# Tile fetches declared free of the scatters of rows that they do not read, in a convolution with a mixture of experts

## The chip, the cores and the metric

The kernel runs on one core of one Trainium2 chip. The metric is the device time of one execution in microseconds (us). Before the change, the median of three runs is 1216.68 us (1212.07 to 1216.96).

## What is computed

There are two parts, one behind the other. The first is a convolution over the sequence with a weight of its own for each position: for 8 x 3584 positions, 8 heads of 24 columns and 7 taps, the softmax over the 7 taps weighs the present row and the 6 before it.

```python
w = softmax(weight_gen)                        # (8, 3584, 8 heads, 7 taps)
out[b, s, h] = sum_k w[b, s, h, k] * x_pad[b, s + k, h]     # 192 columns
```

The second is a mixture of 8 experts over the 28672 rows that result. Each row goes to the one expert whose embedding it is closest to.

```python
logits = normalized(x) @ normalized(expert_emb).T / tau
e = argmax(logits);  gate = softmax(logits)[e]
out = gate * (relu(x @ w1[e]) @ w2[e])         # 192 -> 1024 -> 192
```

## The kernel before

**Units and groups.** The 28672 rows come in 32 units of 896 rows (128 partitions x 7 rows). VectorE forms the seven taps of a unit (`taps`), ScalarE squares, scales and splits the rows into two halves of 16 bits (`squares`, `scale`, `split`), and the result lies in one of three buffers `row_0x` to `row_2x`, unit n in buffer n mod 3. SyncE turns the buffer with a transposing DMA (`turn`, tile `xT`), TensorE forms the logits from it, VectorE picks the expert (`choose`), TensorE counts ranks (`ranks`), and VectorE gives every row its place (`places`). Units are routed in 18 groups: the first four have one unit each, the other fourteen two.

**Lists.** In device memory there is a table `lst` with a region for each expert. `scatter` (line 629) writes the rows of a group to their places with indirect DMAs from POOL, 128 rows each: 7 for a unit, 14 for a group of two. Each expert's list only grows: rows of a later group lie above those of an earlier one.

**Tiles.** The rows are then read back sorted by expert. After most groups a batch of eight tiles is planned, one for each expert, of 128 rows ('P') or 256 rows ('T'): the first batch follows group 1 and reads rows of groups 0 and 1, the second follows group 3, and from group 4 on there is one batch a group. That makes 16 batches, 128 tiles; 28 last tiles follow. `schedule` sets the first row of each tile from what has been placed so far. `fetch` (line 687) reads a register with the row, then issues two DMAs from SyncE: a transposing one that brings the rows in as columns (`xt`, three buffers), and a small one for row numbers and gates (`meta`). TensorE multiplies by the first layer (`first`, into `h_ps`), ScalarE and VectorE or TensorE make the rectified halves `hi` and `lo`, TensorE multiplies by the second layer (`second`, into `acc`), ScalarE scales it into `o`, and POOL stores it by row number (`store`).

**Order.** A planner in the program (`run_steps`, line 1029) lays all steps of all engines out in one order by costs and due times that are written down in the configuration. It calls each step's function in that order, and each engine runs its instructions in the order in which they were called. Scatters of a later group stand on POOL in between the stores; fetches stand on SyncE in one queue with the loads of `x_t` and `w_t` and the turns `xT`. SyncE issues one after the other and stops where one has to wait.

**Waits.** The framework draws an edge from an instruction to earlier ones that write what it reads. A scatter and a fetch both address `lst` by a register or by indices, so for the framework each touches the whole table. By hand, scatters are freed of each other and of the fetches (group "rows" and group "loads", lines 640 to 642). A fetch is given edges to the scatters of its batch's groups by hand as well: `deps`, which for a batch holds the scatters of the groups that no earlier batch has taken. Fetches of earlier batches stand ahead of it in the same queue.

Of the kernel before, what the change touches and what calls it, by code (L numbers as in the profile page):

```python
# [24 lines left out]
    groups=(1, 1, 1, 1, 2, 2, 2, 2, 2, 2, 2, 2, 2, 2, 2, 2, 2, 2),  # L25
# [55 lines left out]
def tile_dynconv_moe(  # L81
# [97 lines left out]
    def raw_ins(i):  # L179
        return getattr(i, "ins", i)  # L180
# [51 lines left out]
    rows = [a[:, 0 : U * ROWP].rearrange("p (t r) -> p t r", r=ROWP) for a in packs]  # L232
# [429 lines left out]
    class Tile:  # L662
# [14 lines left out]
        def load_rows(self, row0, deps):  # L677
            def fetch():
                return self.fetch(nc.sync.value_load(row0, min_val=0, max_val=DUMMY))

            for i in SP.behind(fetch):
                i = raw_ins(i)
                tc.add_to_no_dep_group("loads", i)
                for d in deps:
                    tc.add_manual_dep(i, d.name, sync_dep, reason="rows of the lists")

# [410 lines left out]
    groups, group_of = [], {}  # L1097
# [574 lines left out]
```

## Time and profile before

| | |
|---|---|
| median of three runs | 1216.68 us |
| the profiled execution | 1221.34 us |
| its span, first to last instruction | 1219.4 us |
| mean granted TensorE clock | 0.971 |
| TensorE busy | 1120.5 us (92%) |
| VectorE busy | 1035.9 us (85%) |
| ScalarE busy | 812.4 us (67%) |
| POOL busy | 623.2 us (51%) |

In the profile PE is TensorE's matmuls, PEld its weight loads, DVE is VectorE, ACT is ScalarE, POOL is GpSimd, SP or SPq is SyncE's queue. A name such as `xt<-lst` says what an instruction writes and reads. All instructions that pass through the helper that keeps the program's order stand at L66, so they are told apart by their tiles. The time in brackets at the end of a timeline row is the idle time of that engine just before it, with what ended it. "DMA xt<-lst" as the one that ended a wait is the landing of a fetch, "DMA lst<-row_2x,pos" that of a scatter. SyncE itself is never counted as busy, so its rows have no such bracket; its waits have a table of their own.

### The profile page before, as it was taken

To read this page: it belongs to the slowest core of one execution; us is meant where nothing else is said; L and a number is where in the kernel's file an instruction comes from. 1 tells how busy PE (TensorE), PEld (TensorE's weight loads), DVE (VectorE), ACT (ScalarE), POOL (GpSimd) and SP (SyncE) were. 2 spreads that over 40 slices of the span, in tenths; PEclk is the share of its full clock that TensorE was granted. 3 is DMA by queue.
4 is the path that set the end of the run, shared out by engine and by line. 5 is a ranking of instruction groups with operands and counts; after the bars stand their busy time and mean duration, and the time that the engine had idled before them with its cause. 6 is when DMAs were issued, how large, how long until landed. Compare 5 with 4: busy or idle time off the path is not lost.

```text
span 1219.4 us, 34694 instructions
## 1 busy us (share of the span) xinstructions
PE 1120.5 (92%) x13318; PEld 987.5 (81%) x13318; DVE 1035.9 (85%) x1561; ACT 812.4 (67%) x2076; POOL 623.2 (51%) x566
## 2 busy tenths in 40 slices
PE   4888678859999999999999999999999999999994
PEld 2444477748898888888988899889999999899994
DVE  8999979999998999999999999999985363348982
ACT  1678657668897988888898777576666444434442
POOL 3135243637675575857567584738554632222331
PEclk9988889979999999999999999999999999999997
DMA  9979245555565756665666663654444522112110
GB/s 260 261 163 230 60 130 142 139 135 144 141 189 104 182 150 132 168 158 158 165 137 174 140 154 99 158 124 135 95 96 98 141 57 54 49 38 50 46 43 23
DMA packets 254495, 156.15 MB, mean 128 GB/s; under 512 B 225005, under 2 KB 238565, under 8 KB 251248
## 3 DMA queue, kind: packets, MB, share of 16 engines
q1 hardware_dynamic: 228656, 94.86, 36.3%
q0 software_dynamic: 25664, 58.98, 15.6%
q8 instruction: 106, 1.74, 0.6%
q14 instruction: 69, 0.57, 0.2%
HBM read 62.20 MB, written 46.45 MB: 89 GB/s over the span
## 4 chain that ended last, share of the span: by engine, by line
PE 77%; DVE 10%; DMA 6%; ACT 3%; issue 1%; POOL 0%; SPq 0%; POOLq 0%; DVEq 0%; ACTq 0%
PE h_ps L66 40%; PE acc L66 35%; DVE acc_0x L66 2%; DMA xt<-lst 2%; DMA w_t<-in_weight_gen_dram 2%; PE g_ps L66 1%; DVE prod_1x L66 1%; DMA xT<-row_2x 1%; DVE acc_1x L66 1%; DVE prod_0x L66 1%; ACT hi L66 1%; PE sums_a L66 1%; ACT sq L66 1%; DVE sums L66 1%; DMA lst<-row_2x,pos 1%
## 5 line engine op out<-in xcount | busy, mean ns | idle before, releaser
L66 PE MATMUL h_ps<-xt,wall 128*128 128x128 f16 (+2 forms) x5120 | 466.3, 252 | 26.7 <-DMA xt<-lst 22.3
L66 POOL DMA_INDIRECT out_dram<-o,meta x228 | 298.7, 1310 | 367.1 <-ACT o L66 216.3
L66 PEld LDWEIGHTS <-wall 128*128 128x128 f16 (+2 forms) x5316 | 390.7, 99 | 107.2 <-issue 39.9
L66 PE MATMUL acc<-wall,hi 128*128 128x192 f16 x3200 | 410.8, 246 | 0.0
L66 PE MATMUL acc<-wall,lo 128*128 128x192 f16 x1600 | 394.2, 246 | 2.0 <-ACT lo L66 1.9
L66 ACT ACTIVATE hi<-h_ps 128x512 f16<-128x512 f32 x456 | 259.4, 599 | 132.2 <-PE h_ps L66 124.3
L66 PEld LDWEIGHTS <-hi 128*128 128x128 f16 x3648 | 328.7, 98 | 10.5 <-issue 2.8
L66 DVE SCALAR_TENSOR_TENSOR lo<-h_ps,hi 128x512 f16<-128x512 f32 x236 | 154.8, 686 | 113.0 <-ACT hi L66 111.6
L66 ACT ACTIVATE o<-acc,meta 128x192 f32<-128x192 f32 x228 | 88.2, 419 | 166.0 <-issue 148.8
L66 PEld LDWEIGHTS <-lo 128*128 128x128 f16 x1824 | 178.7, 98 | 3.1 <-ACT lo L66 3.1
L66 DVE TENSOR_TENSOR prod_1x<-x_t,w_t 128x1344 f32<-128x1344 f32 x93 | 144.0, 1548 | 0.0
L66 DVE TENSOR_TENSOR prod_0x<-x_t,w_t 128x1344 f32<-128x1344 f32 x93 | 143.9, 1547 | 0.0
L66 ACT ACTIVATE lo<-h_ps 128x512 f16<-128x512 f32 x220 | 127.5, 600 | 10.2 <-PE h_ps L66 9.7
L66 POOL DMA_INDIRECT lst<-row_0x,pos x77 | 102.2, 1328 | 57.3 <-issue 27.5
L66 POOL DMA_INDIRECT lst<-row_1x,pos x77 | 103.2, 1340 | 34.7 <-issue 29.2
L66 POOL DMA_INDIRECT lst<-row_2x,pos x70 | 89.5, 1279 | 49.6 <-issue 48.8
L66 PE MATMUL h_ps<-hi,minus 128*128 128x512 f16 x220 | 73.1, 380 | 5.9 <-ACT hi L66 5.6
L66 DVE TENSOR_TENSOR acc_0x<-acc_0x,prod_1x 128x1344 f32<-128x1344 f32 x45 | 69.8, 1551 | 0.5
L66 DVE TENSOR_TENSOR acc_1x<-acc_1x,prod_1x 128x1344 f32<-128x1344 f32 x45 | 69.6, 1547 | 0.5
L66 DVE TENSOR_TENSOR acc_0x<-acc_0x,prod_0x 128x1344 f32<-128x1344 f32 x45 | 69.8, 1550 | 0.0
L66 DVE TENSOR_TENSOR acc_1x<-acc_1x,prod_0x 128x1344 f32<-128x1344 f32 x45 | 69.6, 1547 | 0.0
L66 PEld LDWEIGHTS <-xT 128*128 128x128 f16 (+1 forms) x918 | 27.5, 97 | 26.4 <-DVE xT L66 9.6
(217 smaller groups left out, 1368.3 us busy)
## 6 DMA issues: line engine op xcount, KB each, us to landing
x_t<-in_x_dram SPq DMA_DIRECT2D x24, 1248.0 KB
w_t<-in_weight_gen_dram SPq DMA_DIRECT2D x16, 392.0 KB
x_t<-in_x_dram SPq DMA_DIRECT2D x8, 672.0 KB
wall<-in_moe_w_dram POOLq DMA_DIRECT2D x7, 768.0 KB
x_t<-in_x_dram SPq DMA_DIRECT2D x8, 504.0 KB
out_dram<-o,meta POOLq DMA_INDIRECT x228
wall<-in_moe_w_dram POOLq DMA_DIRECT2D x7, 512.0 KB
wall<-in_moe_w_dram POOLq DMA_DIRECT2D x14, 256.0 KB
```

The lines of the kernel that those rows point to most:

```text
L66: self.last = self.tc.keep_in_program_order(op(*args, **kwargs))
```

## The change

One line is added in the function that issues a tile's fetch. Both DMAs of a fetch are declared to have no edge to any scatter issued so far (group "rows"), except those in `deps`. The writes of padding rows behind the lists' ends are in that group too. The edges of `deps` stay, and nothing else in the program is touched.

```diff
             for i in SP.behind(fetch):
                 i = raw_ins(i)
                 tc.add_to_no_dep_group("loads", i)
+                tc.declare_no_dep(i, group="rows", keep=deps, reason="rows of later groups lie above those that are read")
                 for d in deps:
                     tc.add_manual_dep(i, d.name, sync_dep, reason="rows of the lists")
```

## Rows read from the trace of the kernel before

**Rows 1.** Stretches: length, busy PE, PEld, DVE, ACT, POOL (instructions), granted clock, DMA share, GB/s
```profile
130.00:160.00 30.00, 16.30 (x209) 13.97 (x207) 29.96 (x48) 17.77 (x47) 11.80 (x11) 0.87 0.42 109
160.00:190.00 30.00, 24.58 (x333) 23.03 (x334) 21.47 (x32) 19.82 (x55) 14.72 (x14) 0.90 0.50 124
300.00:400.00 100.00, 97.18 (x1205) 86.65 (x1202) 94.75 (x122) 83.44 (x227) 64.04 (x54) 0.98 0.60 150
1000.00:1100.00 100.00, 100.00 (x1169) 92.13 (x1168) 39.06 (x64) 43.27 (x96) 24.62 (x25) 1.00 0.21 49
```
**Rows 2.** Waits between 130 and 255 us: us in total, times, longest
```profile
PE h_ps L66 <- DMA xt<-lst: 12.6, 3, 7.5
...
PE g_ps L66 <- DMA xT<-row_1x: 8.7, 1, 8.7
DVE fr L66 <- PE g_ps L66: 6.3, 1, 6.3
...
DVE row_1x L66 <- ACT row_1x L66: 2.1, 1, 2.1
```
**Rows 3.** Waits of TensorE between 255 and 950 us, same columns
```profile
PE h_ps L66 <- DMA xt<-lst: 9.7, 5, 2.9
PE g_ps L66 <- DMA xT<-row_2x: 2.1, 2, 1.1
...
PE g_ps L66 <- DMA xT<-row_0x: 0.9, 1, 0.9
```
**Rows 4.** Waits of SyncE's queue over the whole span, same columns
```profile
SPq L66 <- PE h_ps L66: 202.4, 81, 6.3
SPq L66 <- DMA lst<-row_2x,pos: 79.7, 19, 7.5
SPq L66 <- DMA lst<-row_1x,pos: 72.1, 21, 7.4
SPq L66 <- DMA lst<-row_0x,pos: 71.2, 22, 8.0
```
**Rows 5.** POOL's timeline: start, us, engine, operation, [idle before it <- released by]
```profile
141.72 1.52 POOL L66 DMA_INDIRECT lst<-row_2x,pos  x1 [25.53 <-issue]
```
**Rows 6.** SyncE's timeline, 140 to 160 us: start, us of issue
```profile
140.69 0.94 SPq L66 DMA_DIRECT2D meta<-lst  x1
...
149.93 0.37 SPq L66 DMA_DIRECT2D x_t<-in_x_dram  x1
158.38 1.24 SPq L66 DMA_TRANSPOSE xt<-lst  x1
```
**Rows 7.** The chain that ended last, 145 to 165 us: start, us, what
```profile
150.10 7.81 DMA lst<-row_2x,pos
```
**Rows 8.** TensorE's timeline, 150 to 167 us
```profile
150.74 2.40 PE L66 MATMUL h_ps<-xt,wall 128*128 128x128 f16 x40
...
162.03 4.30 PE L66 MATMUL h_ps<-xt,wall 128*128 128x128 f16 x40 [7.47 <-DMA xt<-lst]
```
**Rows 9.** TensorE's timeline, at 257 us
```profile
257.01 0.82 PE L66 MATMUL h_ps<-xt,wall 128*128 128x256 f16 x3 [2.92 <-DMA xt<-lst]
```
**Rows 10.** Timelines of SyncE, POOL, TensorE and VectorE, 367 to 375 us
```profile
367.56 1.21 SPq L66 DMA_TRANSPOSE xt<-lst  x1
...
367.55 0.11 POOL L66 MEMSET row_0x<- 128x7 int32 x1 [2.11 <-DMA lst<-row_0x,pos]
...
370.17 3.87 PE L66 MATMUL h_ps<-xt,wall 128*128 128x128 f16 x40 [2.36 <-DMA xt<-lst]
...
374.12 0.16 DVE L66 TENSOR_TENSOR fr<-fr,g_ps 128x8 f32<-128x8 f32 x1 [2.30 <-PE g_ps L66]
```
**Rows 11.** SyncE's timeline, 513 to 518 us
```profile
513.80 0.41 SPq L66 DMA_DIRECT2D meta<-lst  x1
514.34 3.50 SPq L66 DMA_TRANSPOSE xT<-row_2x  x1
```

## The prediction

> **What bounds the kernel now.** I read the page first, then busy time by stretch, then the waits, and last the timelines of the engines around the few places where TensorE stands still. From 300 us on TensorE is busy for 97 of 100 us, and from 1000 us without a break; VectorE has 95 of 100 us in the middle and only 39 of 100 near the end [rows 1]. So TensorE sets the end, and what it loses before is lost for good, unless VectorE holds it up there anyway. Early it is otherwise: between 130 and 160 us TensorE is busy for 16.3 of 30 us and VectorE for 29.96; between 160 and 190 us VectorE too has 8.5 us of idle time [rows 1].
>
> The waits say what part of this is about the fetches of rows. TensorE waits for fetched tiles for 12.6 us in 3 pieces between 130 and 255 us, the longest 7.5, and for 9.7 us in 5 pieces between 255 and 950 us [rows 2, 3]: 22.3 us in all. SyncE's queue, which issues the fetches, waits far longer: 79.7 + 72.1 + 71.2 = 223.0 us in 62 pieces for scatters to land, and 202.4 us in 81 pieces for TensorE, which must have done with a tile before its buffer can be filled again [rows 4]. Most of the 223 us costs nothing, since a fetch runs up to two tiles ahead of its use.
>
> Which scatters are waited for? The first batch of eight tiles reads rows of groups 0 and 1. POOL stood idle for 25.5 us before the scatter at 141.72 [rows 5], which reads row_2x and is the first of group 2: what the batch reads was out long before. Yet its fourth fetch leaves SyncE at 158.38 us, when a scatter that had taken 7.81 us from its issue at 150.10 landed, and TensorE begins on that tile at 162.03 us, having stood for 7.47 us [rows 6 to 8]. That wait is not for data.
>
> **The change, part by part.** No instruction is added, removed or moved: the planner's inputs are untouched, so each engine's order should stay; only edges of the fetches go. Each fetch keeps the waits for its own batch's scatters, for its buffer, and for its place in SyncE's queue.
>
> *The first stall.* SyncE is done with the second tile's metadata at 141.63 us (140.69 + 0.94) [rows 6]. The third tile finds a free buffer (there are three), so its fetch and metadata can be out by about 145.5, the x load, today at 149.93, by 146, and the fourth fetch by 146.5 (an estimate from issue times of 1.24 and 0.94 us a pair [rows 6], with over 1 us to spare). At the 3.65 us of before (158.38 to 162.03) [rows 6, 8] it lands near 150.2; TensorE wants it at 154.56 (162.03 - 7.47). So the 7.47 us go. The stall also has a tail: the 40 matmuls behind it took 4.30 us, against 2.40 us for the 40 at 150.74 [rows 8]; the mean granted clock is 0.90 in 160 to 190 and 1.00 in 1000 to 1100 [rows 1], so part of the stretch runs at the lower of the two levels (1.2 for 2.4 GHz), behind a TensorE that had been idle.
>
> What these 9.4 us are worth is VectorE's to decide, since TensorE's next large stop, 8.7 us for a turned row [rows 2], ends with work of VectorE. VectorE's own waits in this stretch are 6.3 us for the ranks, which TensorE computes behind the late tile, and 2.1 us for ScalarE, which had stood for the same tile [rows 2]. I take 6.3 and half of 2.1: 7.4 us. Bounds: 6.3 from below; from above TensorE's own losses, 12.6 for all three pieces (two shorter ones are of this kind) [rows 2]. I take a value near VectorE's rows because it is the busier engine there. What is late next is the last scatter of group 4, which the tile at 257.01 truly reads: 2.92 us of TensorE idle [rows 9] that stay, only earlier.
>
> *The late stalls.* Of the 9.7 us after 255 [rows 3], 2.92 are that tile's own. The other four pieces, 6.8 us, are tiles near the end of their batches. One of them, the 2.36 us before 370.17, as an example: its fetch leaves at 367.56, in the instant in which POOL's memset of row_0x was released by a scatter out of row_0x [rows 10]; POOL scatters group 6 there, the tile belongs to group 5. VectorE waits behind it too, 2.30 us for the ranks at 374.12 [rows 10], so both engines gain. I take 6.8; bounds 0, and 6.8 with one slow tail of 1.9.
>
> *What stands behind a fetch in SyncE's queue.* The turn of a row for the logits goes out at 514.34 us, directly behind a fetch pair [rows 11], and TensorE then waits for turned rows of this kind: 2.1 us in 2 pieces and 0.9 us in one, 3.0 us [rows 3]. With the fetch earlier, the turn goes out once VectorE has made the row. I take 3.0; bounds 0 and 3.0. All other fetches and loads come earlier into slack that is there today; where it is gone, the next wait is the tile buffer, and that is no stall while TensorE is at work on a tile.
>
> *A load in flight.* The scatter of 7.81 us went out beside an x load (149.93) [rows 6, 7]; the fetch that the wait kept until that load was over took 3.65. In the changed kernel fetches follow x loads closely. If such a fetch takes 7.81 us, the fourth lands at 154.3, still before 154.56; the one at 367.56 would leave soon after 360 and land at 368.5, where TensorE wants it at 367.8, and about 1 us of its 2.36 stays. For two places of this kind I take 2 us off; bounds 0 and the 6.8 of the late stalls.
>
> The Trainium skill ("DMA: Bandwidth & Descriptors", section "Queues, rings and completion order") says that each DMA engine takes a ring's descriptors in order and alternates between the rings packet by packet. The row of 7.81 us agrees with it for a scatter beside a load; for a fetch behind a load on SyncE's own ring no row here shows it. By that rule these 2 us stay off; by the fetch's row alone nothing would.
>
> Sum: 7.4 + 6.8 + 3.0 - 2 = 15.2 us. The profiled execution took 1221.34 us (span 1219.4 and 1.9 around it), so one like it comes to 1206.1; it lies 4.7 us above the median of the runs shown, 1216.68, so for that median 1201.5.
>
> **Rivals.** *A, only the first stage pays.* VectorE, at 95 of 100 us [rows 1], is the true pace in the middle, and what TensorE gains there it spends before turned rows. For it: TensorE's waits for turned rows [rows 3]. Against it: VectorE itself waits for TensorE's ranks at 374.12 [rows 10]. Then 7.4 us remain: 1209.
>
> *B, the wait changes its name.* The fetch waits as long for its buffer or its own scatters, or the program keeps an equal edge by another way. For it: 202.4 us of waits for buffers stand beside the 223 [rows 4]. Against it: at 158.38 us two buffers had long been free. Time: 1214 to 1219.
>
> *C, needed scatters get late (slower).* Loads and fetches leave in the midst of POOL's scatters, which then land as late as the one at 150.10. The place is the first fetch of each of the 16 batches, which truly reads the last scatter. Price: 7.81 - 3.65 = 4.2 us a batch whose slack is used up, as it was at 257.01 [rows 7 to 9]. Four such batches (16.8 us) eat the gain, from six on it is slower by over 0.5%; at eight, 1201.5 + 33.6 = 1235. Against it: the bytes are the same and shift by a few us, and only one of today's stalls is of this kind. By the rule of the Trainium skill named above, scatters and loads share the engines, which is how this rival would come about.
>
> **How the numbers follow.** About 0.5%, 6 us, is what can be told from no change here. Forecast 0.62 (a gain of 10 to 24 us), A 0.18, B 0.13, C 0.07. Faster by over 0.5%: 0.62 and most of A, 0.76; within it: the rest of A and B, 0.17; slower: C, 0.07. The low end, 1191, is the early bound with all later terms and some slow tails (12.6 + 6.8 + 3.0 + 3.3 = 25.7); the high end, 1214, takes in A and the near edge of B.
>
> **What would show it.** Right: SyncE's waits for scatters fall from 223 us to under 50; the first batch's fourth fetch leaves near 146 us; VectorE's 6.3 us wait for the ranks is gone; TensorE's waits for fetched tiles fall from 22.3 to about 5 us, among them the piece at 257.01, then near 249; the span is near 1204. Wrong: stalls of the same size under another name (B), TensorE standing longer before turned rows between 255 and 950 us (A), new waits before the first tiles of batches (C). If the order of instructions changes on any engine, the working is void.

## The result, and the profile after

The changed kernel takes 1196.6 us (median of 4 runs, 1193.47 to 1197.47) against 1214.38 us beside it (1211.65 to 1216.96): ratio 0.9849, 95% interval [0.9816, 0.9883]. A second set, run beside the experiments, gave 1195.76 against 1216.03 us, ratio 0.9832 [0.9804, 0.9859]. The profiled execution took 1197.47 us, with a span of 1195.4 us and a granted clock of 0.976. Every engine runs the same instructions in the same order as before; only waits differ.

The same stretches as in [rows 1]: length, busy PE, PEld, DVE, ACT, POOL (instructions), granted clock, DMA share, GB/s.

```profile
130.00:160.00 30.00, 21.76 (x291) 19.29 (x291) 29.96 (x49) 21.50 (x56) 11.81 (x11) 0.89 0.51 118
160.00:190.00 30.00, 24.91 (x349) 22.32 (x347) 29.91 (x39) 22.07 (x60) 16.67 (x15) 1.00 0.67 158
300.00:400.00 100.00, 99.59 (x1227) 89.08 (x1226) 98.03 (x127) 87.55 (x235) 67.13 (x57) 1.00 0.67 159
1000.00:1100.00 100.00, 100.00 (x1269) 94.45 (x1267) 52.40 (x91) 42.87 (x95) 25.89 (x25) 1.00 0.20 47
```

VectorE no longer has a gap between 160 and 190 us (29.91 of 30, 21.47 before), and TensorE is busy for 99.59 of 100 us from 300 us on (97.18 before).

The waits that answer to [rows 2], 130 to 255 us (us in total, times, longest). The last line is VectorE's only wait there:

```profile
PE g_ps L66 <- DMA xT<-row_1x: 11.5, 1, 11.5
...
PE h_ps L66 <- DMA xt<-lst: 3.4, 1, 3.4
...
DVE row_0x L66 <- DMA out_dram<-o,meta: 0.5, 1, 0.5
```

Between 255 and 950 us TensorE has two kinds of wait left, and neither is for a fetch or for a turned row [rows 3]:

```profile
PE h_ps L66 <- ACT lo L66: 0.9, 2, 0.6
...
PE h_ps L66 <- ACT hi L66: 0.3, 1, 0.3
```

SyncE's queue over the whole span, to set beside [rows 4]:

```profile
SPq L66 <- PE h_ps L66: 323.6, 96, 6.4
...
SPq L66 <- DMA lst<-row_0x,pos: 11.1, 6, 3.5
SPq L66 <- DMA lst<-row_1x,pos: 4.7, 2, 4.3
SPq L66 <- DMA lst<-row_2x,pos: 3.4, 6, 1.5
```

Its waits for scatters fell from 223.0 to 19.2 us; those for TensorE, which must be done with a tile buffer, grew from 202.4 to 323.6. On SyncE the wait did take another name. On TensorE it did not come back, because a fetch that waits for its buffer is two tiles early.

The first stall, SyncE's timeline (start, us of issue), then TensorE's:

```profile
140.56 1.23 SPq L66 DMA_DIRECT2D meta<-lst  x1
142.54 1.21 SPq L66 DMA_TRANSPOSE xt<-lst  x1
...
144.48 0.37 SPq L66 DMA_DIRECT2D x_t<-in_x_dram  x1
145.66 1.30 SPq L66 DMA_TRANSPOSE xt<-lst  x1
```
```profile
150.62 2.40 PE L66 MATMUL h_ps<-xt,wall 128*128 128x128 f16 x40
154.28 2.40 PE L66 MATMUL h_ps<-xt,wall 128*128 128x128 f16 x40
...
242.26 0.89 PE L66 MATMUL g_ps<-enT,xT 128*128 128x16 f16 x27 [11.53 <-DMA xT<-row_1x]
246.52 1.89 PE L66 MATMUL h_ps<-xt,wall 128*128 128x256 f16 x8 [3.37 <-DMA xt<-lst]
```

The fourth fetch leaves at 145.66 us, not 158.38, and lands at 153.45 (read from the landing marks in the trace); TensorE takes the tile at 154.28 us without a wait, and its 40 matmuls last 2.40 us, not 4.30 [rows 6, 8]. The tile that needs the last scatter of group 4 still costs 3.37 us (2.92 in [rows 9]), 10.5 us earlier.

Where the 24.0 us between the two profiled spans arose shows in the start of each unit's logits, which come in the same order in both (my table, from TensorE's timelines):

| unit | before, us | after, us | shift |
|---|---|---|---|
| 3 | 135.1 | 135.0 | -0.1 |
| 4 | 178.9 | 169.7 | -9.2 |
| 5 | 202.2 | 193.2 | -8.9 |
| 7 | 253.2 | 242.3 | -10.9 |
| 8 | 276.1 | 264.7 | -11.4 |
| 11 | 360.9 | 349.5 | -11.4 |
| 12 | 391.6 | 376.0 | -15.5 |
| 16 | 494.1 | 476.9 | -17.2 |
| 18 | 546.1 | 527.7 | -18.4 |
| 22 | 647.7 | 628.2 | -19.5 |
| 27 | 803.7 | 781.4 | -22.3 |
| 31 | 933.7 | 909.7 | -24.0 |

It is a staircase. From unit 8 on each step stands at a place where TensorE had stood in before, and nothing is given back between steps; ahead of it the shift is once 0.3 us smaller, from unit 4 to unit 5. That profile of before was one of the slower executions, so its staircase is higher than the 17.8 and 20.3 us by which the medians differ.

### The profile page after: what moved, and what is told of

It reads as the page before. It is cut to its first block, busy times and chain, and to the rows that moved or that the text cites. A ratio compares the mean times of both kernels' runs of the same rounds, so it can differ in the third digit from the quotient of the medians.

```text
span 1195.4 us, 34677 instructions
## 1 busy us (share of the span) xinstructions
PE 1112.6 (93%) x13318; PEld 982.1 (82%) x13318; DVE 1034.4 (87%) x1561; ACT 811.0 (68%) x2076; POOL 623.7 (52%) x566
## 3 DMA queue, kind: packets, MB, share of 16 engines
q0 software_dynamic: 25664, 58.98, 16.7%
## 4 chain that ended last, share of the span: by engine, by line
PE 78%; DVE 12%; issue 3%; DMA 2%; ACT 2%; POOL 1%; DVEq 0%; POOLq 0%; SPq 0%; ACTq 0%
PE h_ps L66 40%; PE acc L66 35%; DVE acc_0x L66 3%; DVE prod_1x L66 2%; DVE prod_0x L66 2%; DVE acc_1x L66 2%; DMA w_t<-in_weight_gen_dram 2%; PE g_ps L66 1%; PE sums_a L66 1%; DMA wlast<-in_moe_w_dram 1%; DVE sums L66 1%; POOL lst L66 1%; ACT hi L66 1%; DVE w_t L66 0%; DVE wall L66 0%
## 5 line engine op out<-in xcount | busy, mean ns | idle before, releaser
L66 PE MATMUL h_ps<-xt,wall 128*128 128x128 f16 (+2 forms) x5120 | 461.2, 251 | 7.8 <-DVE sums L66 3.4
L66 PEld LDWEIGHTS <-wall 128*128 128x128 f16 (+2 forms) x5316 | 386.0, 98 | 85.7 <-issue 38.0
```

What stands on the lines that cost most here:

```text
L66: self.last = self.tc.keep_in_program_order(op(*args, **kwargs))
```

## The experiments

The question is whether the places add up, and what an edge on one fetch is worth when its neighbours keep theirs. The gated kernels count the fetches in the order of SyncE's queue, from 0 on (against the kernel before; the reason is left out):

```diff
+            k = fetched[0]
+            fetched[0] += 1
             for i in SP.behind(fetch):
                 i = raw_ins(i)
                 tc.add_to_no_dep_group("loads", i)
+                if k < 16:
+                    tc.declare_no_dep(i, group="rows", keep=deps, reason=...)
```

**The first 16 fetches alone** (`k < 16`).

> Only the fetches of the first two batches (tiles 0 to 15) are declared free, the other 140 keep the waits of before. Theory P (each place where a fetch's wait reached TensorE or VectorE pays by itself, and the places add up): in the two profiles the logits of unit 7 begin 10.9 us earlier in the changed kernel, so the gain here is about 11 us, 1203 us (1200 to 1206), and TensorE's waits for fetched tiles between 255 and 950 us stay near 9.7 us. Rival R (all of the gain is made early, the late stalls only follow from the early one): 1197, as fast as the full change. Rival L (VectorE gives the early gain back later): within 3 us of before, 1214.

Measured: 1205.1 us against 1216.36, ratio 0.9919 [0.9896, 0.9942]. From unit 3 to unit 7 its logits gain 11.0 us on before (-2.3 to -13.3), as in the full change. TensorE's waits for fetched tiles between 255 and 950 us are still there. They are 4.6 us, where before's profile had 6.8 without the tile that needs its scatter (9.7 - 2.92; it now lies ahead of 255 us):

```profile
PE h_ps L66 <- DMA xt<-lst: 4.6, 4, 2.9
```

In its profile the shift still grows from -13.7 to -18.1 us behind unit 11, though these fetches keep their waits: there the profile of before had lost more at the same places.

**All fetches but the first 16** (`k >= 16`).

> Only the fetches from tile 16 on are declared free; the first two batches keep their waits. Theory P: the 7.5 us stall before the fourth tile stays, the late stalls and the longer waits for turned rows go: 17.8 - 10.9 = 6.9 us by the medians, 13.1 us by the two profiles, so 1201 to 1208, middle 1205. Rival R (all of the gain is made early): 1214, no change. Rival L (all of it late): 1197.

Measured: 1204.82 us, ratio 0.9912 [0.9889, 0.9936]. Its waits for fetched tiles between 130 and 255 us:

```profile
PE h_ps L66 <- DMA xt<-lst: 15.9, 7, 6.9
```

Behind 255 us it has none, and from there its shift against before goes from -4.1 to -16.7 us: 12.6, as in the full change (-11.4 to -24.0). The two parts lose 0.0081 and 0.0088 of the time, together 0.0169; the full change of the second set loses 0.0168. They add up within the intervals, each some 0.0025 wide to either side, or 3 us, so no sign is left that one part feeds on the other.

**Seven fetches alone** (`k in (3, 7, 14, 31, 45, 86, 99)`), and **the fourth alone** (`k == 3`).

> Only seven of the 156 fetches are declared free, those before which TensorE stood in the profile of before for a scatter that the tile did not need (tiles 3, 7, 14, 31, 45, 86, 99). Theory P: nearly the whole gain except the waits for turned rows (3.0 us): 14 us, 1200 us (1197 to 1204). Rival Q (what pays is that SyncE's whole queue runs earlier; with a few freed, the fetch or the metadata ahead of it in the queue still waits, or the next tile does): less than half of the gain, 1206 or more.

> Only the fourth fetch is declared free. Theory P: the 7.47 us stall goes, with its slow tail; VectorE's split of unit 4 is 8.7 us earlier in the full change, so 8 to 9 us, 1206 us (1204 to 1209); TensorE's pieces before the 8th and the 15th tile (2.6 and 2.5 us) stay or grow by what was won. Rival G (what is won at the fourth tile is waited for again at the 8th and 15th, whose scatters then land no earlier): under 4 us, 1211 or more.

Measured: the seven 1204.91 us, 0.9919 [0.9894, 0.9943]; the fourth alone 1213.9 us, 0.9981 [0.9962, 0.9999]. Both are misses for theory P: the seven give 11.5 us where 14 were expected, between the ranges of P and Q; the fourth gives 2.5 where 8 to 9 were expected, and its interval reaches from 0.1 to 4.6 us. The chain that ended last, with the fourth alone freed (start, us, what), says why. Below it are two rows of SyncE's timeline and one of TensorE's:

```profile
142.53 2.89 DMA lst<-row_2x,pos
145.43 0.02 issue
145.44 3.06 DMA xt<-lst
...
148.64 7.51 DMA xt<-lst
156.15 0.05 issue
156.20 3.81 PE h_ps L66 x34
```
```profile
147.41 0.36 SPq L66 DMA_DIRECT2D x_t<-in_x_dram  x1
148.64 1.47 SPq L66 DMA_TRANSPOSE xt<-lst  x1
```
```profile
156.20 4.45 PE L66 MATMUL h_ps<-xt,wall 128*128 128x128 f16 x40 [3.84 <-DMA xt<-lst]
```

The third fetch still waits for a scatter until 145.43 us. The freed one stands behind it in SyncE's queue, then behind an x load, and needs 7.51 us where the third needed 3.06. So 3.84 of the 7.47 us stay, and the 40 matmuls behind them are still slow (4.45 us). Rival G had the size (under 4 us) but not the reason: the loss is at the fourth tile itself, not at the 8th or 15th. In the kernel with seven freed the same tile waits 4.40 us. Its shift grows by 4.4 us from unit 3 to unit 7 (10.8 in the full change) and by 8.5 us from unit 8 to the end (12.6).

**Fifteen fetches**: the seven, the one ahead of each, and tile 4 (`k in (2, 3, 4, 6, 7, 13, 14, 30, 31, 44, 45, 85, 86, 98, 99)`).

> Fifteen fetches are declared free: the seven tried before (tiles 3, 7, 14, 31, 45, 86, 99), the one ahead of each in SyncE's queue, and tile 4, whose fetch leaves at 156.5 us and would be the next late one. Theory Q (a freed fetch still stands behind the wait of the one ahead, and then directly behind an x load, which costs it 4 us more): the early gain is whole, the turns are not, 15 to 17 us, ratio 0.986 to 0.988. Rival S (many small waits make the rest, the pairs are no better than the seven alone): 0.991 to 0.992.

Measured: 1200.19 us, 0.9874 [0.9849, 0.9899], as theory Q said: about 5.5 us better than the seven (0.0045 x 1216). What is left to the full change is 4.4 us by the medians. The early gain is whole in its profile (10.7 us from unit 3 to unit 7), in spite of a wait of 1.8 us for a tile at 222 us. From unit 8 to the end it gains 9.2 us where the full change gains 12.6: it still waits for turned rows (0.8 and 0.7 us) and for one tile (1.3 us). The rest, some 1 us, is not explained.

**The full change again.**

> The full change once more, for a median beside the experiments and a second profile. The first two batches alone gave a ratio of 0.9919, the rest alone 0.9912. Theory P (the two parts add up): 0.983, 1196 us (1193 to 1199). Rival L (part of the early gain is spent later): above 0.986, 1200 or more.

Measured: 1195.76 us, 0.9832 [0.9804, 0.9859]; its profile follows the first one, 0.6 us ahead from unit 8 to the end.

**More work on VectorE, early and in the middle** (against the full change; `again` holds for units 5, 6, 7 or for units 18, 19, 20).

```diff
                 yield
                 tap(prods[i], k + i, u, x_t, w_t)
+            if again and k == 1:
+                tap(prods[1], 2, u, x_t, w_t)
```

> The full change, and VectorE forms one tap of units 5, 6 and 7 a second time (the same product into the same place, 3 x 1.55 = 4.65 us more work on VectorE between 160 and 235 us). Theory V (with the early stalls gone VectorE sets the pace up to the turned row of unit 7, where TensorE waits 11.5 us): 4.65 us slower than the full change, ratio near 0.987. Rival T (TensorE or the loads set the pace there): 0 to 1 us, as the full change.

> The full change, and VectorE forms one tap of units 18, 19 and 20 a second time (4.65 us more work on VectorE between 490 and 565 us). Theory V (from 300 us on TensorE sets the pace; the turned rows of these units land 2.2 to 4.2 us before TensorE takes them): 0 to 1.5 us slower than the full change, the first wait before a turned row at unit 19 or 20. Rival A (VectorE, 98 of 100 us busy there, is the pace in the middle): 4.65 us slower.

Measured: early 1199.82 us, 0.9864 [0.9839, 0.9889], 4.1 us over the full change beside it; in the middle 1197.54 us, 0.9851 [0.9827, 0.9875], 1.8 us over it. Early the added work comes back almost whole (in the profiles 4.7 us from unit 3 to unit 7), so VectorE sets the pace there. In the middle less than half of it does, somewhat more than theory V's 1.5 us at most. The wait before a turned row that was expected there does not show; TensorE's only new wait in that kernel is for VectorE's counts, at 512 us:

```profile
PE g_ps L66 <- DVE cnt L66: 1.3, 1, 1.3
```

At units 18 to 20 VectorE thus had about 3 us (4.65 - 1.8) to spare over three units: TensorE is the pace there, but not by much.

**Only the transposing half of each fetch**, and **two softmax steps on POOL**. The first cut is against the kernel before, the second against the full change. Four runs follow: the transposing half; the softmax steps on POOL in the old order; the same with POOL's cost told to the planner, which then makes a new order; and the second one again.

```diff
-            for i in SP.behind(fetch):
+            for j, i in enumerate(SP.behind(fetch)):
...
+                if j == 0:
+                    tc.declare_no_dep(i, group="rows", keep=deps, reason=...)
```
```diff
-                lazy(lambda rows=rows: softmax(ins[c, None], rows)),
+                lazy(lambda rows=rows: softmax(ins[c, None], rows, G_ if c in (2, 3) else SM)),
```

> All 156 transposing fetches are declared free, but not the metadata behind them: the wait for scatters moves from a fetch to its metadata, where nothing on TensorE needs it soon. Theory Q (SyncE's queue passes a wait on to what stands behind): the fourth fetch leaves behind the third tile's metadata (scatter landed at 145.4 us when only the fourth was free) and behind an x load, lands near 156 us, and about 4 us of TensorE's stall stay; late, a fetch is held by the wait of the tile ahead, which ends some us sooner than its own: half of the late gain and of the turns or more. Ratio 0.986 to 0.990, 1202 us. Rival M (only a fetch's own wait counts): 0.983, 1196. Rival N (a pair is as late as either half): above 0.995.

> The full change, and the two wide steps of the softmax of units 4 to 7 (4 of 0.97 us) go to POOL instead of VectorE, at the same places of the order. Theory V (VectorE sets the pace up to unit 7's turn): up to 3.9 us faster than the full change, ratio 0.980, if POOL has the results in time. Rival W (POOL is slower at them and they stand among its scatters, so VectorE waits for POOL and the needed scatters land later): same or up to 4 us slower, 0.983 to 0.987.

> As the kernel before this one, but the planner knows of it (POOL at 1.83 us each) and lays the whole order out anew. Theory V: 3 to 4 us faster than the full change, ratio 0.980. Rival W: POOL's scatters get later, 0.983 to 0.987. A new order can bring late stalls of its own: if it is over 0.987, the waits between 255 and 950 us show whether that is why.

> The kernel with the two wide softmax steps of units 4 to 7 on POOL, same order, once more, since TensorE and its weight loads stood for waits that the profile can't name in all kernels of the last runs (131.6 us in 331 pieces before weight loads, 55.2 in 197 in the full change before), so that VectorE didn't set the early pace there. Theory V: up to 3.9 us faster than the full change (0.9832), 0.980. Rival W (VectorE waits for POOL's slower steps, needed scatters land later): 0.983 to 0.987.

These four ran on two other chips than the experiments above. Every kernel took some 7% longer there, the one before too (1305.28 and 1302.35 us), and none has the full change beside it, so only ratios are given. The transposing half alone: 0.9879 [0.9819, 0.9940]. Its chain has the predicted row, a fourth fetch that leaves behind metadata and x load and lands at 156.46 us:

```profile
148.84 7.62 DMA xt<-lst
156.46 0.05 issue
156.51 2.41 PE h_ps L66 x40
```
```profile
156.51 2.41 PE L66 MATMUL h_ps<-xt,wall 128*128 128x128 f16 x40 [0.86 <-DMA xt<-lst]
```

On SyncE's queue this is theory Q's picture. TensorE, though, stood for only 0.86 us where about 4 were expected: it came to the tile at 155.65 us, against 152.36 with the fourth alone freed. Behind 255 us it waits for no fetched tile. The interval reaches M's ratio too, so this run does not decide between Q and M. The softmax on POOL in the old order: 0.9910 [0.9874, 0.9947] and 0.9888 [0.9838, 0.9937]; in a new order 0.9979 [0.9948, 1.0010]. Nothing there is better than the full change's 0.9832, but the sets can't be compared closely: TensorE's weight loads stood for something that the profile doesn't name, 55.2 us over the whole span in the second profile of the full change and 131.6 in the transposing half:

```profile
PEld L66 <- issue: 55.2, 197, 4.2
```
```profile
PEld L66 <- issue: 131.6, 331, 3.8
```

The cause is not known, and whether POOL could relieve VectorE early stays open.

## Why the prediction was right

The forecast was 1201.5 us, 15.2 us under before; the medians say 1196.6 and 17.8, the second set 20.3. The mechanism came out, but the closeness is in part luck. The sum was read from a profile, and between the two profiled executions the gain is 24.0 us: the span was forecast near 1204 and is 1195.4. The medians moved by less, since that execution of before lay 7.0 us above the median beside the result. Against the profile 8.8 us are missing from the sum, 4.0 early, 2.8 late and the 2 taken off. Step by step:

- **The order stays.** It did.
- **The fourth fetch leaves near 146 us.** It left at 145.66, and the 7.47 us went whole. It took 7.8 us to land, not the 3.65 of this step; the paragraph on loads in flight had allowed for that, with a landing at 154.3, and it landed at 153.45.
- **7.4 us early.** Measured 10.9 (unit 7), 11.4 by unit 8, and 11.0 with the first 16 fetches alone (unit 3 to unit 7). That VectorE decides was right: more work on it comes back, and TensorE now waits 11.53 us for unit 7's turned row where it waited 8.72. The size was off in the step "6.3 and half of 2.1". VectorE has 0.5 us of waits left in the stretch, so all of before's went: the 6.3, the whole 2.1 [rows 2] and two smaller kinds, 1.4 and 1.0, which the sum left out, 10.8 together. Here the engine that sets the pace got back every wait that it had. The two kinds in before, 130 to 255 us:

```profile
DVE row_2x L66 <- ACT row_2x L66: 1.4, 2, 0.8
DVE rz L66 <- ACT sc L66: 1.0, 1, 1.0
```

- **6.8 us of late stalls.** All four went, one of them with a slow tail: the step at unit 12 is 4.1 us for a wait of 2.36 [rows 10], since the 40 matmuls behind it had taken 3.87 us where 2.40 is usual, at a granted clock of 0.66 from 370 to 375 us. Behind two others of the four the matmuls were at full pace, with a granted clock of 1.00:

```profile
475.86 2.41 PE L66 MATMUL h_ps<-xt,wall 128*128 128x128 f16 x40 [1.47 <-DMA xt<-lst]
...
775.29 1.29 PE L66 MATMUL h_ps<-xt,wall 128*128 128x128 f16 x20 [2.66 <-DMA xt<-lst]
```

- **3.0 us of turns.** Gone. The turn at 514.34 us [rows 11] no longer stands directly behind a fetch pair; it goes out 19.6 us earlier, while the work around it is 17.2 us earlier (unit 16):

```profile
494.72 3.48 SPq L66 DMA_TRANSPOSE xT<-row_2x  x1
```

Late stalls and turns make 12.6 us between 255 us and the end (-11.4 to -24.0). The waits themselves are the 9.8 that were predicted; the other 2.8 are 1.8 in the slow stretch at unit 12, inside the upper bound of the late stalls (one slow tail of 1.9), and 1.0 of slightly longer busy time at the six other pieces (my sums over TensorE's timelines).

- **2 us off for loads in flight.** This step was wrong, by place and not by mechanism. A fetch behind an x load can take as long as the scatter of [rows 7]: 7.51 and 7.62 us in the chains above. For the fourth tile that was foreseen to fit, and it did. For the tile of [rows 10] I let only its own fetch move, to soon after 360 us. In the changed kernel the fetch and the x load ahead of it leave earlier too: it goes out at 347.23 us, lands at 353.33, and TensorE takes the tile at 356.25 without a wait. Of the 156 fetches, 28 leave while an x load is in flight, 13 in before; they take 5.5 us in the median where the others take 3.1 (counted over the trace), and none of these is late. The Trainium skill ("DMA: Bandwidth & Descriptors", section "Queues, rings and completion order") has each DMA engine take a ring's descriptors in order, and these durations agree with it. The 2 us did not come out, since the tiles had slack.
- **Rival A** is refuted after 255 us by the second experiment, which frees only the late fetches and gains there, and by VectorE's added work in the middle, which came back by less than half. **Rival B** happened on SyncE alone (323.6 us). **Rival C** did not: the only wait for a fetch before a batch's first tile is the old one, 3.37 us.

## What to carry to other kernels

When an engine's queue waits for things that it does not need, remove the wait from the whole queue: freeing only the instruction that is seen to be late leaves it behind its neighbours' waits, and here gave 2.5 of some 19 us. To size the gain, take the pacing engine's own waits in each stretch, all of them, and add the slow matmuls behind those stalls after which the granted clock is low. A fetch issued behind a bulk load took nearly twice as long here (5.5 for 3.1 us), which cost nothing because it left early enough. A sum read from one profile belongs to that execution: set it beside the profile after the change, and not only beside the medians.

## What the runs showed of the hardware that was not expected

- Runs of before scatter over 5.3 us beside the result (4 runs) and over 9.5 and 11.3 us beside the experiments (11 and 17 runs), those of the full change over 4.0 and 2.3 (4 and 5 runs). That the removed waits hung on when other transfers landed would explain it, and the first experiment's late waits, 4.6 us for 6.8 with the same fetches held, point that way; it is not shown.
- Of the two longest of the four late stalls the shorter was followed by slow matmuls (2.36 us, granted clock 0.66 behind it), the longer was not (2.66 us, 1.00). Why is not known.
- A wide softmax step that takes VectorE 0.97 us took POOL 2.0 us (mean of 4, with the softmax steps on POOL in the old order).
